# Transposing the first two x tiles by DMA instead of on TensorE

## The chip, the cores and the metric

One core of a Trainium2 chip. The metric is device time in microseconds (us). A profile's span is about 1.6 us shorter than the time of the run that it comes from.

## The reference, cut to what matters

```python
x = A_x                                                  # 1 x 2048 x 1024, bf16
g = sigmoid((x * gate_w).sum(-1, keepdims=True))
a = linear_attention(x, A_wqkv, A_wo)                    # qkv = x @ wqkv, 32 heads
b = x with one row (the argmax of x @ w_r) passed through a gated FFN and added back
return g * a + (1 - g) * b
```

Every product with x needs x transposed (the 1024 features on the partitions). The x tiles are 128 rows each, t = 0 to 15; W_k is loaded in eight chunks of 128 features, k0 to k7.

## The kernel before: the parts that matter

Tiles 2 to 15 of x are already transposed on their way from memory. Tiles 0 and 1 are loaded plainly and transposed on TensorE, because TensorE can start on them early (at 3.88 and 6.36 us).

```python
N_WARM = 6
def load_x(t0, n):                                       # plain load of n tiles
    xt4 = xin.tile([P, n, D], BF, name=f"xnat{t0}", bufs=1)
    sp.dma_start(out=xt4[:, 0:n, :], in_=x_v[:, t0 : t0 + n, :])
    ...
load_x(0, 1); load_k(0); load_x(1, 1)                    # one queue, in this order
for c in range(1, KC): load_k(c)
sp.dma_start(out=wkv[:, :, v_cut : 2 * D], in_=...)      # the V tail: the last 320 columns of W_v
for t in (2, 3):
    sp.dma_start_transpose(out=xT[:, :, t * P : (t + 1) * P], in_=x2d[t * P : (t + 1) * P, :])
for g4 in range(1, 4):                                   # 512 rows each
    sp.dma_start_transpose(...)
...
warm(N_WARM)                                             # matmuls on constants, until x0 is there
unit_T(0)                                                # 8 transposes, 2 copies to xT
warm(3, 128)
first_mm(0, 0, 1)                                        # tile 0 x k0: two matmuls, 512 columns
pe.transpose(wps[:], wrg_rows[:], ...)                   # router and gate weights
unit_T(1)
for c in range(1, KC):                                   # thirty matmuls: k1..k7 for both tiles, k0 for tile 1
    first_mm(0, c, c + 1)
    if c < KC - 1: first_mm(1, c - 1, c)
... first_mm(1, 6, 8)
for t in range(3): unit_V(t, 2, ...)                     # "ps" matmuls with the V tail
```

Later, four times, unit_KVACC for four tiles runs as a block of 128 tiny matmuls (33 columns), each with its own weight load: the "KV accumulation" below.

## Time and profile before

| | before |
|---|---|
| time, median of 3 runs | 249.49 us (248.97 to 249.51) |
| span of the profile | 247.7 us |
| TensorE (PE) busy | 242.3 us, 98% |
| VectorE, ScalarE busy | 70%, 52% |
| mean DMA rate from 2 to 7 us | 292 GB/s |

TensorE is busy almost from the first microsecond to the last, so time is lost or won only where its run starts, breaks or slows down. The chain of waits and the timeline of the first 14 us are shown in the prediction. Two more lines of the chain, which gave nothing away at the time, are needed later: the second and the third KV accumulation, with the start in the first column.

```profile
83.96 1.33 PE kvacc L83 x128
...
123.43 1.27 PE kvacc L83 x128
```

### The profile page before, as it was taken

The numbers are of one execution on the slowest core, as the hardware profiler recorded it, in microseconds if no ns is written. First come the engines' busy times: TensorE is split into PE (matmuls) and PEld (weight loads), VectorE is DVE, ScalarE is ACT, GpSimd is POOL, SyncE is SP. The second block draws the span as 40 slices with busy tenths as digits, with TensorE's granted clock in tenths as the row PEclk, the third lists the DMA queues.
The fourth block names the chain that finished last, engine by engine and source line by source line (L and its number), as shares of the span: only waits on it lengthen the run. The fifth ranks groups of instructions, "written<-read, shape, count | busy, mean of one in ns | idle before, by whom it ended". The sixth has DMA issues, their size and how long they took to land.

```text
span 247.7 us, 4893 instructions
## 1 busy us (share of the span) xinstructions
PE 242.3 (98%) x1923; PEld 123.6 (50%) x1923; DVE 172.7 (70%) x264; ACT 127.6 (52%) x215; POOL 52.6 (21%) x100
## 2 busy tenths in 40 slices
PE   7999999999999999999999999999999999999994
PEld 3465756754554554554554555544443444444442
DVE  0043125279985879845989999996779999954342
ACT  3095434456565466544565555668887633333300
POOL 6000000300000100000013300101666689950000
PEclk9999999999999999999999999999999999999999
DMA  6999994399969992589659892000004654564122
GB/s 193 352 229 201 260 393 157 101 337 335 275 178 314 343 288 76 155 294 396 227 166 425 298 252 58 3 2 24 0 3 127 196 181 155 150 192 168 47 83 86
DMA packets 46311, 47.78 MB, mean 193 GB/s; under 512 B 16776, under 2 KB 35472, under 8 KB 46224
## 3 DMA queue, kind: packets, MB, share of 16 engines
q1 hardware_dynamic: 45648, 46.28, 61.1%
q0 software_dynamic: 608, 1.19, 1.8%
q8 instruction: 15, 0.25, 0.4%
q14 instruction: 8, 0.07, 0.1%
q10 hardware_dynamic: 32, 0.00, 0.0%
HBM read 39.33 MB, written 8.39 MB: 193 GB/s over the span
## 4 chain that ended last, share of the span: by engine, by line
PE 95%; DMA 2%; SPq 1%; DVE 0%; issue 0%; DVEq 0%
PE ps L83 88%; PE first L83 3%; PE kvacc L83 2%; DMA wkv<-in_A_wqkv_dram 2%; PE red L83 1%; PE dps L83 1%; PE pm L83 1%; SPq L83 1%; DVE ot L83 0%; PE yps L83 0%; DVEq L737 0%; PE pt L83 0%; PE hps L83 0%; PE rps L83 0%; PE xs_ps L83 0%
## 5 line engine op out<-in xcount | busy, mean ns | idle before, releaser
L83 PE MATMUL ps<-wkv,xT 128*128 128x352 bf16 (+2 forms) x608 | 106.5, 334 | 0.0
L83 PEld LDWEIGHTS <-xT 128*128 128x128 bf16 x640 | 62.2, 98 | 49.3 <-issue 0.6
L83 ACT ACTIVATE u<-ps 128x512 f32<-128x512 f32 x60 | 35.9, 598 | 46.4 <-PE ps L83 46.2
L83 PE MATMUL ps<-xT,wq 128*128 128x512 bf16 x256 | 58.4, 379 | 0.0
L83 PE MATMUL ps<-m_sb,pq_all 128*128 128x512 bf16 (+2 forms) x264 | 55.6, 373 | 0.0
L83 ACT ACTIVATE e<-u 128x512 f32<-128x512 f32 x64 | 40.3, 630 | 2.0
L83 PEld LDWEIGHTS <-pq_all 128*128 128x128 bf16 x264 | 25.4, 98 | 30.2 <-issue 0.7
L640 POOL TENSOR_TENSOR pq_all<-pq_all,rb 128x512 bf16<-128x512 bf16 x32 | 36.5, 1166 | 12.1 <-DVE rb L83 11.7
L83 PEld LDWEIGHTS <-wq 128*128 128x128 bf16 x256 | 24.4, 98 | 28.4 <-issue 1.4
L83 DVE SCALAR_TENSOR_TENSOR gacc<-wt,hcol,gacc 128x1024 f32<-128x1024 bf16 x27 | 34.5, 1279 | 0.4
L83 DVE SCALAR_TENSOR_TENSOR ot<-ps,gate,xg 128x512 bf16<-128x512 f32 (+2 forms) x33 | 23.5, 723 | 14.3 <-PE ps L83 14.2
L83 DVE SCALAR_TENSOR_TENSOR gacc<-wt,xs_f,gacc 128x2048 f32<-128x2048 bf16 x14 | 32.8, 2346 | 0.2
L83 ACT ACTIVATE xg<-xt,omg 128x1024 f32<-128x1024 bf16 x16 | 18.1, 1146 | 26.9 <-DVE ot L83 25.9
L83 DVE SCALAR_TENSOR_TENSOR pq_all<-ps,e 128x512 bf16<-128x512 f32 x32 | 21.9, 686 | 11.3 <-ACT e L83 11.3
L83 DVE SCALAR_TENSOR_TENSOR pk<-ps,e 128x512 bf16<-128x512 f32 x28 | 19.1, 686 | 11.8 <-ACT e L83 11.8
L83 DVE STREAM_SHUFFLE rb<-rdp 128x512 f32<-128x512 f32 x32 | 22.5, 731 | 0.0
L83 ACT CAST vt<-ps 128x352 bf16<-128x352 f32 x32 | 14.4, 453 | 11.5 <-PE ps L83 11.1
L214 POOL MEMSET vt<- 128x22 bf16 x16 | 3.8, 441 | 75.8 <-PE kvacc L83 75.3
L83 ACT CAST vc<-ps 128x320 bf16<-128x320 f32 x16 | 6.5, 428 | 7.3 <-PE ps L83 7.3
L83 DVE COPY rg<-ps 128x2 f32<-128x2 f32 x16 | 2.5, 159 | 10.2 <-ACT vc L83 10.1
L355 POOL DMA_DIRECT2D xs<-in_A_x_dram x1 | 0.7, 711 | 39.8 <-DVE sig L83 39.8
L83 DVE SCALAR_TENSOR_TENSOR pk<-first,e 128x512 bf16<-128x512 f32 x4 | 2.8, 692 | 8.2 <-ACT e L83 8.2
(100 smaller groups left out, 94.0 us busy)
## 6 DMA issues: line engine op xcount, KB each, us to landing
wt<-in_B_w_down_dram SPq DMA_DIRECT2D x14, 512.0 KB, 5.5
wt<-in_B_w_gate_dram SPq DMA_DIRECT2D x8, 512.0 KB, 7.4
wt<-in_B_w_up_dram SPq DMA_DIRECT2D x8, 512.0 KB, 6.4
xt<-xp SPq DMA_DIRECT2D x16, 256.0 KB, 2.6
out_dram<-ot SPq DMA_DIRECT2D x15, 256.0 KB, 2.0
wt<-in_B_w_gate_dram SPq DMA_DIRECT2D x8, 384.0 KB, 7.8
wt<-in_B_w_up_dram SPq DMA_DIRECT2D x8, 384.0 KB, 7.1
wkv<-in_A_wqkv_dram SPq DMA_DIRECT2D x8, 256.0 KB, 5.1
```

Of the source, the lines that this page charges most:

```text
L83: inst = fn(*a, **k)
L214: nc.gpsimd.memset(vt_t[t][:, :, 32:33], 1.0)
L355: nc.gpsimd.dma_start(out=xs8[:], in_=x2d[bass.ds(idx_val, 1), :].rearrange("o (c p) -> (o c) p", p=P))
L640: nc.gpsimd.tensor_tensor(sl, sl, rb[:], op=ALU.mult)
```

## The change

Its intent: take the last x transposes and their copies off TensorE, VectorE and ScalarE, and let all of x arrive transposed. The warm-up is lengthened to bridge the wait for x0.

```diff
-N_WARM = 6
+N_WARM = 8
...
-    load_x(0, 1)
+    load_xt(0)          # dma_start_transpose of 128 rows, straight into xT
     load_k(0)
-    load_x(1, 1)
+    load_xt(1)
     for c in range(1, KC):
         load_k(c)
...
-    unit_T(0)
-    warm(3, 128)
     first_mm(0, 0, 1)
-    wps = ps_ffn.tile([P, 16], BF, tag="f")
+    wps = ps_t.tile([P, 16], BF, tag="t")
     pe.transpose(wps[:], wrg_rows[:], ident[0:16, 0:16])
     dve.tensor_copy(wkv[:, :, 2 * D : 2 * D + 2], ...)
-    unit_T(1)
+    warm(2, 128)
     for c in range(1, KC):
         first_mm(0, c, c + 1)
```

TensorE's instruction stream shrinks by 30 instructions: the traces record 1923 weight loads before and 1908 after, each with one matmul. (The expectations below count 3803 and 3773; these totals stand in no trace, and only the difference of 30 is used.)

More of the change, by code (lines that the diff above doesn't have):

```diff
@@ L124, with load_xt @@
     wrg_rows = xin.tile([16, P], BF, name="wrg_rows", bufs=1)
-    xnat = {}
-    def load_x(t0, n):
-        xt4 = xin.tile([P, n, D], BF, name=f"xnat{t0}", bufs=1)
-        sp.dma_start(out=xt4[:, 0:n, :], in_=x_v[:, t0 : t0 + n, :])
-        for i in range(n):
-            xnat[t0 + i] = xt4[:, i, :]
     def load_k(c):
         sp.dma_start(out=wkv[:, c, 0:D], in_=wqkv_v[:, c, D : 2 * D])
-    load_x(0, 1)
+    def load_xt(t):
+        sp.dma_start_transpose(out=xT[:, :, t * P : (t + 1) * P], in_=x2d[t * P : (t + 1) * P, :])
+    load_xt(0)
     load_k(0)
-    load_x(1, 1)
+    load_xt(1)
     for c in range(1, KC):
@@ L198, in phi_evac @@
         phi_dve(ps, phi_exp(ps), out_ap)
-    def unit_T(t):
-        for h, eng in enumerate((dve.tensor_copy, act.copy)):
-            pst = ps_t.tile([P, 512], BF, tag="t")
-            for c in range(4):
-                pe.transpose(pst[:, c * P : (c + 1) * P], xnat[t][:, (4 * h + c) * P : (4 * h + c + 1) * P], ident[:])
-            eng(xT[:, 4 * h : 4 * h + 4, t * P : (t + 1) * P], pst[:].rearrange("p (c s) -> p c s", c=4))
     pk_t = {}
```

## The prediction

> **What bounds the kernel now.** I read the page first (TensorE busy 98% of the 247.7 us span), then the chain of waits, then the order of time of the first 36 us on TensorE and on the DMA queue of SyncE, then DMA rates in short stretches. All rows show start and duration in us.
>
> The chain that ended last, its first pieces in order of time:
>
> ```profile
> 0.98 0.40 SPq L83
> ...
> 1.45 0.42 SPq L83
> ...
> 1.90 0.45 SPq L83
> ...
> 2.40 4.73 DMA wkv<-in_A_wqkv_dram
> 7.13 0.04 issue
> 7.17 6.64 PE first L83 x30
> 13.81 22.67 PE ps L83 x152
> ```
>
> After 7.17 us nearly every later piece is TensorE, without a gap. What the change can move is therefore when that unbroken run starts. The run starts when the second K weight chunk (call it k1, issued fourth on the queue at 2.40) lands at 7.13. The issue slots of the three loads ahead of it are on the chain too.
>
> The timeline of TensorE before that moment:
>
> ```profile
> 1.02 2.72 PE L83 MATMUL warm_ps<-const-bfloat16-1.0 128*128 128x512 bf16 x6 [1.02 <-PEq L726]
> ...
> 3.88 1.03 PE L83 MATMUL pst<-ident,xnat 128*128 128x128 bf16 x8
> 4.71 0.53 PE L83 MATMUL warm_ps<-const-bfloat16-1.0 128*128 128x128 bf16 x3
> ...
> 5.03 0.85 PE L83 MATMUL first<-wkv,xT 128*128 128x512 bf16 x2
> ...
> 6.36 0.62 PE L83 MATMUL pst<-ident,xnat 128*128 128x128 bf16 x8 [0.37 <-DMA xnat<-in_A_x_dram]
> ...
> 7.17 6.64 PE L83 MATMUL first<-wkv,xT 128*128 128x512 bf16 x30 [0.19 <-DMA wkv<-in_A_wqkv_dram]
> ```
>
> The 16 x transposes (rows pst) end at 6.98 and TensorE then waits 0.19 us for k1. So the transposes lie in the shadow of the weight load, if only just: removing them alone cannot start the run before 7.13.
>
> The queue's timeline for the transposing DMAs that the kernel already has (128 rows, 128 rows, then 512 rows), and DMA rates (last two columns: share of 16 engines, GB/s) in a stretch of plain loads and a stretch of transposes alone:
>
> ```profile
> 7.15 3.97 SPq L83 DMA_TRANSPOSE xT<-in_A_x_dram  x1
> 11.17 1.75 SPq L83 DMA_TRANSPOSE xT<-in_A_x_dram  x1
> 12.97 4.48 SPq L83 DMA_TRANSPOSE xT<-in_A_x_dram  x1
> ```
> ```profile
> 9.00:10.00 1.00, 1.00 (x7) 0.41 (x5) 0.00 (x0) 0.00 (x0) 0.00 (x0) 1.00 1.04 398
> 22.00:23.00 1.00, 1.00 (x10) 0.71 (x8) 0.04 (x1) 0.97 (x3) 0.00 (x0) 1.00 1.27 290
> ```
>
> A transposing DMA moves 290 GB/s where a plain load moves 398, and it holds the queue for 1.75 to 3.97 us per 128 rows where a plain load of the same 256 KB holds it for 0.40 to 0.45. The issue list gives 4.3 us from issue to landing for the one at 11.17, against 2.8 us for the first plain x load on an empty queue and 4.4 us for the second.
>
> [...] The trace shows 219 to 314 ns each on TensorE, pipelined to 8 in 0.62 us when warm; no record isolates one 128x128 block by DMA. [...] The first x load here, issued from SyncE, took 2.8[...]. [...] the warm-up matmuls and the first two real ones start 0.43 us apart, the thirty after 7.17 take 6.64/30 = 0.22 us each. The clock rose somewhere between.
>
> **The change part by part.**
>
> *Removed from TensorE, VectorE and ScalarE.* 16 transposes (1.03 + 0.62 us) and 3 narrow warm-ups, with 4 copies to SBUF (0.42 us each on VectorE, 0.58 on ScalarE). All before 7.13, where TensorE waits for k1 anyway; VectorE and ScalarE are then idle. Worth at most the 0.19 us slack turned the other way: gain 0.
>
> *Two more warm-ups (6 to 8), and two narrow ones later.* 8 x 0.43 = 3.4 us from 1.02, so to 4.45. They end before x and k0 are there: cost 0.
>
> *The queue order.* It stays x0, k0, x1, k1..k7, V tail, transposes. Two plain x loads become transposes ahead of k1. Two costs follow.
> (a) Issue. Is the 1.75 us real work or back-pressure? At the end of the issues at 7.15, 11.17 and 12.97 I count from the packet records about 1,500 packets issued and not yet moved each time, so the queue looks full and the issue blocked by it. On the empty queue at 0.98 two issues of 64 packets per DMA engine should be shorter. I take 0.4 us (as a plain load) as the floor and 1.75 as the ceiling: k1's issue moves from 2.40 to between 2.4 and 2.40 + 2 x (1.75 - 0.43) = 5.0.
> (b) Movement. 256 KB at 290 instead of about 395 GB/s is 0.90 against 0.66 us: 2 x 0.24 = 0.5 us more ahead of k1. The rate also falls for up to half a microsecond at the end of each transpose in the fine windows, so up to 1 us.
> With short issues k1 lands at 7.13 + 0.5 to 1.0 = 7.6 to 8.1. With long issues the engines have already worked off what lay ahead, and k1 takes about the 2.85 us of a nearly empty queue: 5.04 + 2.9 = 7.9. Both meet near 8.0: **+0.85 us**. x0 is there by about 4.7 (issue end 2.73 plus the 2.0 us from issue end to landing of the last two large transposes), x1 by about 7: ahead of k1, so they set nothing.
>
> *Clock.* TensorE now idles from 4.45 until about 5.5, does two matmuls, one tiny transpose and two narrow warm-ups, and idles again until 8. [...] Each cold matmul costs 0.21 us[...]. I give it a 30% chance and a typical loss of 1 us: **+0.3 us**.
>
> *Later transfers.* The V tail lands at 6.33 + 6.9 = 13.2 and is wanted at 13.64: slack 0.45. The first 512-row transpose lands at 12.97 + 8.1 = 21.05 and is wanted about 21.5: slack 0.4. Both shift by the extra movement (0.5 to 1.0 us), and TensorE's need shifts by 0.85: slack kept on average, a chance of 0.3 us lost. I add **+0.1**.
>
> Sum: 0 + 0.85 + 0.3 + 0.1 = +1.25 us. TensorE has no idle time later that could absorb it, so it arrives in full at the end: 249.49 + 1.25 = 250.7.
>
> **The rivals.**
> 1. *The first transposing DMA is dear in itself.* The 3.97 us issue at 7.15 was the first of its kind; if its extra 2.2 us is a first-use cost and not the full queue, x0's issue ends at 4.95, k1 is issued at about 7.2 and lands at about 10.1: +3 us, and with TensorE cold after a long idle +4 to +5. For it: it is the first. Against it: the packet count above. Result 252.5 to 254.5; 10%.
> 2. *Hidden anyway.* If empty-queue issues are short and the engines are not yet the limit that early, k1 lands where it did, and the removed 0.2 us wait and copies balance the rest: 249.2 to 249.8. For it: only 300 GB/s moved from 3.8 to 7.1, below the 395 that the engines can do. Against: the transposes use more DMA engine time per byte. 20%.
> 3. *A gain.* It needs k1 to land earlier than 7.13, and nothing was taken from ahead of it on the queue. A gain of 5 us (2%) has no source, since all of the start before 7.17 is only 7 us and most of it is transfer.
>
> **Range and chances.** The body of the estimate is +0.5 to +1.8; rival 2 sets the low end and rival 1 the high end. Predicted **250.7 us**, 8 in 10 between **249.3** and **252.6**. Two per cent is 5 us: faster 0.01, slower 0.04, within 0.95.
>
> **What would show it.** In the profile after: no pst rows; the chain of waits still begins on the queue and reaches TensorE's unbroken run through the landing of k1, at about 8.0 instead of 7.13; the queue rows of the first two transposes last between 0.4 and 1.75 us each; the thirty matmuls still take about 6.6 us if warm, more if cold; the chain from there to the end is as long as before (240.5 us). I am wrong if the first transpose holds the queue for 4 us, if x0 or x1 lands after k1 and becomes the wait, if the thirty matmuls take 8 us or more, or if new waits for the V tail or the 512-row transposes appear between 13 and 31 us.

## The result, and the profile after

255.08 us median (254.47 to 255.52, 4 runs) against 249.23 for the kernel before (4 runs): ratio 1.0234, 95% interval 1.0204 to 1.0265. The change made the kernel slower by over 2%, and the time lies outside the predicted range. (Measured again later, the lower end of the interval was 1.0181, so "over 2%" holds for these rounds and "about 2%" for both.)

The chain of waits of the changed kernel, in order of time (start, duration, what):

```profile
0.98 1.36 SPq L83
...
2.41 0.56 SPq L83
...
3.02 1.24 SPq L83
...
4.31 5.22 DMA wkv<-in_A_wqkv_dram
9.57 9.23 PE first L83 x30
18.80 4.59 PE ps L83 x33
...
89.07 1.35 PE kvacc L83 x128
90.42 0.32 PE ps L83
90.75 1.12 issue
...
129.63 1.27 PE kvacc L83 x128
```

Three things differ from the chain before. The thirty matmuls start at 9.57 instead of 7.17. They last 9.23 us instead of 6.64. And after the second KV accumulation stands a gap of 1.12 us put down to "issue": TensorE waited for nothing that the profile shows. Starts of the same pieces of work, one beside the other, split the loss without remainder:

| start of | before | after | shift | added here |
|---|---|---|---|---|
| the thirty matmuls | 7.17 | 9.57 | 2.40 | 2.40 |
| the "ps" run behind them | 13.81 | 18.80 | 4.99 | 2.59 |
| second KV accumulation | 83.96 | 89.07 | 5.11 | 0.12 |
| third KV accumulation | 123.43 | 129.63 | 6.20 | 1.09 |
| end of the span | 247.7 | 254.0 | 6.3 | 0.1 |

The granted TensorE clock (the share of its full speed that TensorE was allowed, in the column before the last two) explains the second row. These are busy times in four stretches of the changed kernel; the first pair of numbers is the stretch and its length, then PE, with the number of instructions in brackets:

```profile
4.70:8.00 3.30, 0.92 (x5) 0.36 (x5) 0.17 (x1) 0.00 (x0) 0.41 (x5) 1.00 1.10 267
8.10:9.50 1.40, 0.00 (x0) 0.00 (x0) 0.00 (x0) 0.00 (x0) 0.00 (x0) 0.50 0.88 294
9.60:14.80 5.20, 5.20 (x13) 1.84 (x13) 0.00 (x0) 0.00 (x0) 0.00 (x0) 0.50 1.22 312
14.90:18.60 3.70, 3.70 (x18) 1.67 (x17) 0.00 (x0) 0.81 (x2) 0.00 (x0) 1.00 1.06 237
```

The clock was full from 4.62 to 8.03, then half until 14.86, then full again: 13 matmuls in 5.2 us at half clock, 18 in 3.7 us at full. From 4.7 to 8.0 TensorE worked 0.92 us of 3.30. Its timeline shows why:

```profile
1.02 3.57 PE L83 MATMUL warm_ps<-const-bfloat16-1.0 128*128 128x512 bf16 x8 [1.02 <-PEq L712]
...
5.99 0.59 PE L83 MATMUL first<-wkv,xT 128*128 128x512 bf16 x2 [1.39 <-DMA wkv<-in_A_wqkv_dram]
...
9.57 9.23 PE L83 MATMUL first<-wkv,xT 128*128 128x512 bf16 x30 [2.67 <-DMA wkv<-in_A_wqkv_dram]
```

TensorE idles 1.39 us before k0 and 2.67 us before k1. In the kernel before, the transposes (1.03 and 0.62 us) filled most of those waits: 0.37 us of idling was left before x1 and 0.19 before k1. They cost no time on the path; that they kept the clock up is what the first two experiments test.

### The profile page after: what moved, and what is told of

It is laid out like the page before. It is cut to its first block, busy times and chain, and to the rows that moved or that the text cites. A ratio compares the mean times of both kernels' runs of the same rounds, so it can differ in the third digit from the quotient of the medians.

```text
span 254.0 us, 4831 instructions
## 1 busy us (share of the span) xinstructions
PE 242.5 (95%) x1884; PEld 123.1 (48%) x1908; DVE 171.9 (68%) x262; ACT 126.6 (50%) x213; POOL 52.6 (21%) x100
## 4 chain that ended last, share of the span: by engine, by line
PE 94%; DMA 2%; SPq 1%; issue 1%; DVE 0%; DVEq 0%
PE ps L83 85%; PE first L83 4%; DMA wkv<-in_A_wqkv_dram 2%; PE kvacc L83 2%; SPq L83 1%; PE red L83 1%; PE dps L83 1%; PE pm L83 1%; DVE ot L83 0%; PE yps L83 0%; DVEq L723 0%; PE pt L83 0%; PE hps L83 0%; PE rps L83 0%; PE xs_ps L83 0%
## 5 line engine op out<-in xcount | busy, mean ns | idle before, releaser
L83 PE MATMUL ps<-xT,wq 128*128 128x512 bf16 x246 | 57.6, 379 | 1.8 <-issue 1.4
L83 DVE SCALAR_TENSOR_TENSOR ot<-ps,gate,xg 128x512 bf16<-128x512 f32 (+2 forms) x33 | 23.9, 735 | 14.3 <-PE ps L83 14.2
L83 PE MATMUL first<-wkv,xT 128*128 128x512 bf16 x32 | 9.8, 475 | 4.1 <-DMA wkv<-in_A_wqkv_dram 4.1
```

What stands on the lines that cost most here:

```text
L83: inst = fn(*a, **k)
```

## The experiments

**Theory after the first look.** Three separate losses: (1) k1 lands late behind transposing DMAs; (2) TensorE idles while it waits and its clock falls to half; (3) 30 fewer instructions bring the gap behind the second KV accumulation. **Rivals:** the clock falls for another reason, such as the transposing DMAs; the gap is chance or belongs to the DMA stream; k1 is late because the transposes hold the queue, not because their data move slowly.

### Keep TensorE busy, and restore the instruction count

```diff
-N_WARM = 8
+N_WARM = 13
     warm(2, 128)
+    warm(10)
```

> The change as it is, plus 15 full warm-up matmuls: 5 more after the first eight (4.6 to 5.7 us) and 10 in the wait for k1 (6.9 to 9.1 us). They keep TensorE busy through the two idle stretches, and they put its instruction count back to that of the kernel before (3803 instead of 3773). Theory: of the 5.85 us lost, 2.4 us is k1 landing late (9.53 instead of 7.13), 2.6 us is the clock falling to half at 8.03 because TensorE idled, and 1.1 us is a stall for instructions at 90.75[...]. Expects 249.2 + 2.4 = 251.4 to 251.9 us, thirty matmuls of 'first' in 6.6 us, no half-clock stretch after 9 us, no gap after the second KV accumulation, k1 still at about 9.5. Rival 1 (the clock fell for another reason than idleness, such as the transposing DMAs): thirty matmuls still 9.2 us, 254 us. Rival 2 (the gap at 90.75 is chance or comes from the DMA stream): gap of 1.1 us stays, 252.7 us.

251.61 us (before on the same chip 249.04; ratio 1.0101, interval 1.0085 to 1.0118). Its chain:

```profile
1.02 5.71 PE warm_ps L83 x13
6.73 0.51 PE first L83 x2
...
7.34 2.41 PE warm_ps L83 x12
9.75 4.53 PE first L83 x21
...
14.34 1.89 PE first L83 x8
16.23 6.32 PE ps L83 x41
```

The 29 recorded matmuls take 6.5 us (16.23 - 9.75 = 6.48): full clock (1.00 granted from 9.8 to 16.0) although the same DMAs run. Both clock and gap rivals fall for the sum, and the time is as expected. That it is so is partly luck: k1 landed at 8.44 here, not 9.5, and my filler ran past it (the chain starts in the warm-ups), so this run carries about 1.2 us of its own making in place of the late landing.

### Restore the instruction count alone

```diff
-N_WARM = 8
+N_WARM = 7
+    warm(16, 16)
     warm(N_WARM)
```

> The change, with 16 tiny warm-up matmuls (16 columns) in place of one of the eight large ones, ahead of the other seven: again 3803 TensorE instructions, but no work in the idle stretches. Theory: only the instruction stall goes, 255.1 - 1.1 = 254.0 us; the thirty matmuls still take about 9.2 us and k1 lands at 9.5. Rival (the gap is chance or from DMA): 255.1 us with a gap near 90.75.

253.09 us (ratio 1.0160, interval 1.0133 to 1.0188). The gap is gone; second and third accumulation are 39.41 us apart, as in the kernel before (39.47), against 40.56 in the changed one:

```profile
87.81 1.28 PE kvacc L83 x128
89.41 0.05 issue
...
127.22 1.27 PE kvacc L83 x128
```

The thirty matmuls still took 9.3 us (8.37 to 17.64 on the chain), as expected, at half clock until 13.74; here the clock had not fallen but had never risen before. k1 landed at 8.33 instead of 9.5, which more than covers the rest of the difference from my 254.0.

### The stall put into the kernel before

```diff
     for g in range(NG):
         for h in range(4):
+            if t == 3 and 4 * g + h >= 17:
+                continue          # 15 tiny matmuls left out at 48 us: wrong result on purpose
             pe.matmul(kv_slot(g)...)
```

> The kernel before with nothing changed but the last 15 tiny matmuls of one KV accumulation at 48 us left out (a wrong result on purpose): 30 TensorE instructions fewer ahead of the second KV accumulation at 84 us, as in the changed kernel, with the same loads and clock. [...] a gap of 1.0 to 1.2 us appears after that accumulation, at about 85 to 87 us, and the time is 249.0 + 1.0 = 250.0 us. If it came from the transposing DMAs, the clock or chance: no gap, 248.9 to 249.1 us.

250.35 us (ratio 1.0054, interval 1.0031 to 1.0078): 15 matmuls less, 1.3 us more (1.0 was expected). Its chain:

```profile
83.58 1.26 PE kvacc L83 x128
...
85.16 1.50 issue
...
124.43 1.27 PE kvacc L83 x128
```

The gap appears in a kernel with plain x loads and full clock (mean granted 1.00); the accumulations are 40.85 us apart. The packet records show what moves: a DMA packet of 16,384 bytes of kind "instruction" starts at 80.81 in the kernel before, 3.2 us ahead of the second accumulation, and likewise 3.4 us ahead in the run above without a gap. In the two kernels with the gap it starts 0.4 us (89.46) and 0.6 us (84.17) into the accumulation and takes 1.15 us. The accumulation is exactly 128 matmuls and 128 weight loads, done in 1.3 us. In all three profiles with the gap (the changed kernel's two and this one) TensorE stops at the same place of its stream, behind the 735th recorded weight load.

That the instruction count decides is shown, by these three runs, and no later run with the count of the kernel before had the gap. That TensorE waits for the late packet was my reading; it is not shown. Two things it leaves open: the packet of the changed kernel ended at 90.61, and TensorE went on only at 91.86; and at the third accumulation the packet was as late (130.73, 1.1 us after its start at 129.63) without a gap.

### The changed kernel again

> The changed kernel, unaltered, beside the others on one chip. If its first profile was typical, k1 lands at 9.5, there is a half-clock stretch of 6.8 us and a gap of 1.1 us after the second KV accumulation, time 255.1 us. The two profiles of the same load order with other TensorE fillers showed k1 at 8.3 to 8.4; if 9.5 was chance, k1 lands at 8.4 here, and the half-clock stretch must be longer or begin at the start for the time to stay at 254.5 to 255.5. The gap should be there every time, since it hangs on the instruction count alone.

254.10 us (ratio 1.0204, interval 1.0181 to 1.0228). Second profile of the unaltered change: k1 lands at 8.88, the thirty matmuls take 8.17 us on the chain with 3.4 us of half clock (8.65 to 12.06), the gap is 1.48 us. The three losses are there again as 1.75, 1.53 and 1.35 us. So the first profile's split was one draw: the sizes vary from run to run, with when the data land and with when the clock changes. The gap was there both times, as expected.

### A filler fitted to k1

```diff
-N_WARM = 8
+N_WARM = 10
+    warm(10, 16)
     warm(N_WARM)
...
     warm(2, 128)
+    warm(3)
```

> The change with TensorE kept busy as in the first experiment, but fitted so that the filler ends before k1 lands (10 tiny, 10 large ahead of x0; 3 large after), instruction count 3803 as in the kernel before. All that is left of the loss is then the late landing of k1 at about 8.4: 249.04 + 1.2 to 1.4 = 250.3 us, thirty matmuls in 6.5 to 6.7 us starting at 8.4. If the clock term had another cause than idle TensorE, the thirty matmuls take over 8 us and the time is above 252.

252.82 us (ratio 1.0140, interval 1.0109 to 1.0171): a miss by 2.5 us. k1 landed at 9.44 this time, so the filler ended 1.7 us early, and the clock fell again:

```profile
5.50:8.70 3.20, 1.70 (x9) 0.61 (x8) 0.18 (x1) 0.00 (x0) 0.00 (x0) 1.00 0.97 268
9.50:12.20 2.70, 2.70 (x7) 0.97 (x7) 0.00 (x0) 0.00 (x0) 0.00 (x0) 0.50 0.97 341
12.30:17.20 4.90, 4.85 (x23) 2.25 (x23) 0.00 (x0) 0.76 (x2) 0.00 (x0) 1.00 1.16 255
```

The gaps were 0.55 and 1.74 us. TensorE was busy for 53% of the first stretch, and that did not hold the clock: 0.50 was granted from 9.5 to 12.2. The expectation's signs of the rival all but came true (the thirty matmuls took 7.98 us on the chain against "over 8", the time is above 252). But TensorE did idle here, so this run does not speak for the rival; the first experiment, where it did not idle, speaks against it.

### Is it the queue or the movement? The transposes on another queue

```diff
 def load_xt(t):
-    sp.dma_start_transpose(...)
+    nc.scalar.dma_start_transpose(...)     # ScalarE's queue; fillers as in the next run
```

> As e1 in instruction count and in keeping TensorE busy (5 more large warm-ups, then 3 large and 7 of 64 columns), but the two x transposes are issued from the ScalarE queue, so k0 and k1 are issued at 0.98 and 1.45 on the SyncE queue without waiting for the transposes' issue. Theory A (k1 is late because the two transposes hold the queue, 1.36 and 1.24 us instead of 0.40 and 0.45): k1 lands at 7.0 to 7.6 and the time is 249.0 to 249.8. Theory B (k1 is late because transposed x moves slowly on the DMA engines): k1 lands at 8.5 to 9.5 or x0 and x1 become late instead, time 250.7 to 251.7.

256.36 us (ratio 1.0312, interval 1.0270 to 1.0354), worse than any. k0 and k1 were issued at 0.98 and 1.45 and k1 landed at 7.16, but x0, issued at 0.98, landed at 7.37 and x1 at 11.94. Moving the issue moved the lateness to x. Part of the 256 is my design's fault: the router weights, issued behind the transposes on ScalarE's queue, landed at 11.68 on the chain. TensorE idled 3.79 us for them, and the clock was at half from 8.56 to 15.39, so this run did not keep TensorE busy as it was meant to. Theory B's alternative clause held, its time did not.

### k1 ahead of x1

```diff
     load_k(0)
+    load_k(1)
     load_xt(1)
-    for c in range(1, KC):
+    for c in range(2, KC):
```

with five more warm-ups first and three large and seven 64-column ones in the wait; the instruction count is that of the kernel before.

> As e3 in TensorE work, all on the SyncE queue, but k1 is issued ahead of the second x transpose: x0, k0, k1, x1, k2. Theory A (issue order): k1 is issued at about 3.0 instead of 4.3 and lands at about 8.0; x1, issued after it, lands at about 8.3 and becomes the wait of the third matmul; time 250.0 to 250.8. Theory B (slow movement on the DMA engines): the four together are done no earlier than 9.2 to 9.5, time as e1, 251.4 to 251.9.

250.66 us (ratio 1.0062, interval 1.0045 to 1.0079). k1 landed at 6.77 and x1 at 7.76, both earlier than either theory said, but now k2, issued at 4.77, landed only at 9.48 and became the wait (0.83 us). The four loads were done at 7.76, 0.7 us sooner than in the first experiment (8.44), and k2 was no sooner (9.10 there). The time is theory A's, and theory B's landing of all four at 9.2 or later is refuted. What remains of B is that k2, the fifth, was no sooner: order shifts who waits, not when the first five loads are all there.

### Half of the change: only x1 by DMA

```diff
 (the kernel before)
-    load_x(1, 1)
+    sp.dma_start_transpose(out=xT[:, :, P : 2 * P], in_=x2d[P : 2 * P, :])
...
-    unit_T(1)
+    warm(8, 256)
```

> Half of the change: x0 loaded plainly and transposed on TensorE as before, only x1 by a transposing DMA; 8 warm-ups of 256 columns stand where its transposes were, so the instruction count is 3803. If each transposing DMA costs its own part of k1's delay (1.2 us for two), k1 lands at 7.6 to 7.8 and the time is 249.6 to 249.9. If the first one carries it all (a cost of starting), k1 is at 7.1 to 7.3 less or no delay here, 249.0 to 249.3; if a drain of the queue around each transpose does, at 8.0 or more, 250.0 or more.

249.67 us (ratio 1.0028, interval 1.0011 to 1.0044). The time is that of the first alternative, k1 (7.23) that of the second, so this run alone decides nothing between them. The clock was at 1.00 in the three stretches read (4.75 to 5.75, 6 to 7, 7.5 to 8.5).

### The other half: only x0 by DMA

```diff
-    load_xt(1)
+    load_x(1, 1)
...
     warm(2, 128)
+    unit_T(1)
+    warm(2)
```

with N_WARM = 13; the instruction count is that of the kernel before.

> The other half of the change: x0 by a transposing DMA, x1 loaded plainly and transposed on TensorE; TensorE kept busy (13 large warm-ups first, 2 after x1's transposes), 3803 instructions. The kernel with only x1 by DMA had k1 at 7.23 and the third chunk k2 at 7.87, no later than in the kernel before (7.85), while both by DMA gave k2 at 9.0 to 10.2. If the transpose at the head of the queue carries the loss (its data start later, and nothing is queued behind it to fill the slump that follows it), k2 lands at 8.8 to 9.4 here and the time is 250.6 to 251.4. If the loss needs two transposes with a plain load between them, k2 lands at 7.9 to 8.3, time 249.6 to 250.2.

250.06 us (before on this chip 249.34, where two of its seven runs took 251; ratio 1.0004, interval 0.9948 to 1.0060). k1 landed at 7.47, k2 at 8.12. My theory that the transpose at the head of the queue carries the loss fell. By the landing of k1, one transpose costs little (0.10 and 0.34 us in these two profiles) and two cost more than twice as much (1.20 to 2.40 us in the five profiles with the changed kernel's load order).

### What a transposing DMA does to the loads behind it

The last three columns of a stretch are granted clock, DMA share and GB/s. First experiment (x0, k0, x1, k1), the three stretches while x1 moves, after it, and later:

```profile
4.75:5.75 1.00, 1.00 (x4) 0.37 (x3) 0.00 (x0) 0.00 (x0) 0.37 (x4) 1.00 1.20 289
6.00:7.00 1.00, 1.00 (x4) 0.29 (x2) 0.00 (x0) 0.00 (x0) 0.00 (x0) 1.00 0.61 61
7.50:8.50 1.00, 1.00 (x8) 0.40 (x5) 0.06 (x1) 0.00 (x0) 0.00 (x0) 1.00 1.05 402
```

Only x1 by DMA, the stretch just behind x1:

```profile
4.75:5.75 1.00, 0.88 (x6) 0.42 (x6) 0.19 (x2) 0.44 (x1) 0.38 (x4) 1.00 0.90 134
```

The kernel before, the same stretch:

```profile
4.75:5.75 1.00, 1.00 (x7) 0.39 (x5) 0.20 (x1) 0.58 (x1) 0.36 (x4) 1.00 0.84 258
```

After the transpose the plain loads, long issued, crawl at 61 or 134 GB/s for up to a microsecond, then run at 402. The changed kernel's own first profile is different, the stretch behind x1 first:

```profile
6.00:7.00 1.00, 0.91 (x5) 0.34 (x5) 0.17 (x1) 0.00 (x0) 0.00 (x0) 1.00 1.15 226
```

Here x1 itself was slow (209 GB/s from 5 to 6 us, against 277 in the first experiment) and landed 0.36 us later. A slump stands only behind x0, 135 GB/s from 4.0 to 4.5. Yet k1 was a microsecond later than in the first experiment, so the slump alone does not set its landing.

Over the whole stretch from 2 to 7 us the DMA engines moved 292 GB/s in the kernel before, 258 and 250 with one transpose, 192 and 193 with two in the changed kernel. Five microseconds at 100 GB/s less are 0.5 MB, or, as an estimate, 1.3 us at the 395 GB/s of the kernel before from 8 to 10 us. But in the first two experiments, where k1 landed earlier, it was 176 and 172, so this rate does not order the runs with two transposes. That the slump's length follows the number of changes from transposed to plain loads was tried with two orders, TensorE kept busy by fillers put ahead of x0:

```diff
-    load_xt(0); load_k(0); load_xt(1)
+    load_xt(0); load_xt(1); load_k(0)      # adjacent
+    load_k(0); load_xt(0); load_xt(1)      # k0 first
```

> The change with both x transposes issued one after the other, then k0, k1: x0, x1, k0, k1; TensorE kept busy by fillers put ahead of x0, 3803 instructions. In the packet records plain loads crawl at about 64 GB/s for 0.7 to 1.0 us after each transpose. If that slump comes at each change from transposed to plain packets, one of two is saved: k1 lands at 7.5 to 8.0, k2 at 8.2 to 8.6, time 250.0 to 250.6. If each transpose brings its own delay wherever it stands, k1 stays at 8.4 to 9.5 and k2 at 9.0 to 10.2, time 251 to 252.

> As the run with adjacent transposes, but k0 ahead of both: k0, x0, x1, k1. If the loss is the slump after a change from transposed to plain packets plus the late start of a queue that begins with a transpose, this order has one slump and no late start: k1 at 7.2 to 7.8, k2 at 7.9 to 8.4, time 249.5 to 250.3. If each transpose brings its own delay, k2 at 9.0 or later, time above 250.8.

250.79 us (ratio 1.0027, interval 0.9973 to 1.0082) and 250.61 us (ratio 1.0022, interval 0.9968 to 1.0077), on the chip with the unsteady kernel before. k1 landed at 8.19 in both, k2 at 8.86 and 8.85: between the two answers. In each profile plain loads follow a transpose in a slump once instead of twice, deep in the first (stretch 5.25 to 6.25 below) and 89 GB/s for half a microsecond in the second. In the first the rate is also low between the two transposes, 146 GB/s from 3.5 to 4.5:

```profile
5.25:6.25 1.00, 0.70 (x4) 0.20 (x2) 0.00 (x0) 0.00 (x0) 0.00 (x0) 1.00 0.63 55
```

So some slump is in every profile looked at with a transpose at the front. That removing one saves time is not shown: 8.19 is 0.14 to 0.25 us earlier than the two earliest of the five profiles in the changed kernel's order, which themselves spread from 8.33 to 9.53. Why the engines crawl, and how k1's delay splits between the slump and the slower transposed packets, stays open.

The kernel before is steadier in k2 than in k1: in the run with 15 matmuls left out, whose loads are the same, k1 landed at 6.37 and k2 at 7.78, against 7.13 and 7.85. The intervals of the last two runs are wide, so they say little of times; and in both the V tail, landing at 15.64 and 14.95, became a wait of its own.

### An attempt to beat both

```diff
 (the kernel before)
     load_k(0)
+    load_k(1)
     load_x(1, 1)
...
+    first_mm(0, 1, 2)
     unit_T(1)
```

> An attempt to beat both: the kernel before with its x transposes on TensorE, but k1 loaded ahead of x1 and the first tile's matmuls with k1 done before x1's transposes; same instructions, same count, other order. k1 then lands at about 6.4 and x1 at 7.1; TensorE does two real matmuls (0.43 us) while it waits for x1, but x1's transposes (0.6 us), which lay in the wait for k1, now lie after it. If these cancel, 248.9 to 249.4 us, the same as before; if waiting for k1 and not for x1 was the bound, 248.5 us.

249.24 us against 249.29 (5 rounds, ratio 1.0000, interval 0.9986 to 1.0015): the two effects cancel. No version tried beats the kernel before.

## Why the prediction was wrong, point by point

- **What bounds the kernel, and the gain of 0 from the removed work: right.** TensorE's run starts with k1, and every shift reached the end in full. The halves of the change, each removing one tile's transposes, gained nothing. (One reading was slightly off: the last copy on ScalarE ran to 7.61, not only to 7.13; nothing waited for it.)
- **Issue, and rival 1: right.** The two transposes held the queue for 1.36 and 1.24 us, inside 0.4 to 1.75; k1 was issued at 4.31, inside 2.4 to 5.0. The first one was not dear, so rival 1's mechanism fell; that the times landed at and just above its range (254.10 and 255.08 against 252.5 to 254.5) is chance.
- **x0 and x1 in time: right.** They landed at 4.46 (predicted 4.7) and 6.94 (7).
- **k1's landing, +0.85: too small.** The step that failed is "k1 takes about the 2.85 us of a nearly empty queue". It took 5.22 us in the first profile and 4.57 in the second: +2.40 and +1.75 (in the five profiles with this load order k1 landed at 8.33 to 9.53, +1.20 to +2.40). The queue was not nearly empty: when k1 was issued at 4.31, x0, k0 and x1 were all still on their way, and x1 landed only at 6.94. What else slowed k1 is open, as said above. The sum also rests on a misreading: "the rate also falls for up to half a microsecond at the end of each transpose". The windows of the kernel before that I had asked for show longer falls around its transposes: 136 GB/s on average from 14.3 to 15.4 us, 83 from 18.8 to 20.7, 127 from 23.9 to 25.2.
- **Clock, +0.3: the largest error.** I saw the idle stretches but gave the loss 30% and 1 us. It was 2.59 and 1.53. The step that failed: I thought only of whether the clock would rise in time. It did rise, at 4.62; then it fell at 8.03, with only two matmuls and a few small ones between two waits (0.92 us busy of 3.41, 27%; with the waits filled, in the first experiment, it did not fall).
- **Later transfers, +0.1: right in that nothing came of it** (no wait for the V tail or the 512-row transposes). The 0.12 before the second accumulation and the 0.1 at the end are not such waits, so the agreement in size is chance.
- **Missing from the sum:** the stall of 1.12 to 1.50 us that a changed instruction count brought. Neither the sum nor any rival named it.
- **Sum:** 1.25 predicted; 2.40 + 2.59 + 0.12 + 1.09 + 0.1 = 6.3 measured on the spans. The 4% for "slower" rested on all three being small together.

## What to carry to other kernels

Work that lies in the shadow of a wait may still hold the clock up (its removal cost 2.59 and 1.53 us at half clock here): before removing it, ask what fills the wait afterwards, and size the filler for the latest landing, not the typical one. A change in the number of instructions can bring a stall far away (30 fewer gave 1.12 to 1.50 us here, behind 128 tiny matmuls), so compare the chain to the end, piece by piece, and test with padding before blaming the change's idea. Transposing DMAs at the very front of a kernel can delay the plain loads behind them by more than their slower rate accounts for: two of them by 1.20 to 2.40 us here, where the rates (290 against 395 GB/s) had given 0.5.
